# Zero matmuls paced by ScalarE, also into the emptied P.V bank, to a higher count; planned slack behind VectorE, GpSimd and DMA inputs

## Chip, cores, metric

One core of one Trainium2 chip. The metric is device time in microseconds (us) of one execution; lower is better. ACT is ScalarE, DVE VectorE, PE TensorE (PEld its weight loads), POOL GpSimd, SP the engine that issues DMAs.

## The reference, cut

Two identical layers on `x` of 2048 x 512 in bf16, each an attention block with 32 query heads of width 16 and one shared key/value head, followed by a gated MLP with a 2048 x 2048 spatial product.

```python
for layer in range(2):
    x = x + A(layernorm(x))   # q = xn@wq (32 heads), k, v shared; softmax(q k^T / 4) v; @ wo
    x = x + B(layernorm(x))   # z = gelu(xn@w_in); z1, z2 = halves; z1 * (w_sp @ layernorm(z2) + b) @ w_out
```

The softmax needs 2 x 32 x 2048 x 2048 exponentials. That is what ACT does for most of the time.

## The kernel before

The program contains a list scheduler. While it is built it simulates all engines with its own estimates of durations, and emits one fixed order of instructions for each engine, with semaphore waits. At run time an engine that must wait in the middle of its order stops everything behind it.

Scores (QK) are made in "fill" steps of two or three blocks of 128 keys x 512 queries, ACT takes the exponential of two or three blocks at a time from PSUM, and P.V adds them up in one bank, `pvb`. A group is 16 units of four blocks; after it, DVE copies the bank out (`oT`), and only then may the next group write it. Every seventh or eighth block goes to DVE instead of ACT, as a chain of six operations. Projections, MLP and spatial products are side work in two spare banks. Some of it passes through DMA transposes.

Since the attention alone loads PE lightly, the scheduler puts in matmuls of zeros ("zeros" below), so that each window of about 3.4 us has enough columns of work for the clock. These are the parts that matter:

```python
TICK = 3.4133
TICK_COLS = 3060.0
WARM = 800.0
# ... (cut) in the scheduler
    def _arm(self, o):        # when an operation's inputs are all planned
        o.ready = max([d.end if d.eng == "pe" and o.eng == "pe" else d.vis for d in o.deps], default=0.0)
# ... (cut)
    def transpose(self, out, src, deps, sem, pr):
        return self.sc.op("sp", lambda e: e.dma_start_transpose(out, src), 1.2, deps, pr, sem=sem, dma=131072, lat=0.9)
# ... (cut)
class WarmStream:
    def peek(self, f):
        # ... (cut)
        t = sc.below(f, TICK_COLS + WARM)        # first time at which the last window holds fewer columns
        if u >= len(k.units) or k.units[u].first:    # P.V of the next unit would clear the bank
            free = [b for b in sc.banks if not b.busy and not b.closed and b.free_at <= t]
            if not free:
                return None
            self.bank = free[0]
        if not sc.fast(t):
            return (t, -1.0)
        return (t, 0.6)

    def commit(self, t):
        # ... (cut)
        def fn(e):            # adds zero to the P.V bank, or writes zeros to a spare bank
            return e.matmul(k.b32(k.pvb if b is None else b.idx), k.zero[:], k.zero[:, None, :].to_broadcast([P, 4, P]),
                            start=b is not None, stop=b is not None)
        pace = []
        if t > k.sc.free["pe"] + 0.3:
            pace = [d for en in ("act", "dve") for d in k.sc.order[en][-8:] if t - 1.5 < d.vis <= t]
            pace = sorted(pace, key=lambda d: -d.vis)[:1]     # wait for the ACT or DVE operation planned to end last
        o = k.sc.op("pe", fn, 512 / 2400.0, [k.c_zero] + pace + (b.rel if b is not None else []), 9.0, sem="warm")
```

The softmax here doesn't subtract the row's maximum and nothing guards it: scores larger than these inputs give would overflow.

## Time and profile before

| | before |
|---|---|
| timed runs known at the prediction | 1846.22 us median of 3 (1843.32 to 1848.53) |
| the profiled execution, not among them | 1860.4 us, span of the core 1858.4 |
| granted clock in the profiled execution | 0.983 |
| zeros / blocks on DVE | 786 / 514 |

The page of before: busy time of each engine, two of its rows of 40 slices (tenths), the chain that ended last by engine, and two groups. A group's line gives its operation and shapes, then busy us, mean ns of one, and the idle time of its engine just before it.

```profile
span 1858.4 us, 30069 instructions
PE 1599.4 (86%) x11874; PEld 473.0 (25%) x11874; DVE 1700.6 (92%) x2912; ACT 1746.0 (94%) x1570; POOL 52.4 (3%) x90
...
ACT  8999999999999999999569999999999999999983
PEclk9899999999999999998999999999999999999999
...
ACT 39%; DVE 21%; PE 20%; issue 17%; DMA 1%; POOL 1%; ACTq 0%; SPq 0%; POOLq 0%
...
L1374 ACT ACTIVATE Pa<-ps_all 128x1536 bf16<-128x1536 f32 (+1 forms) x1433 | 1631.8, 1372 | 32.6 <-PE ps_all L1694 30.8
...
L1676 PE MATMUL ps_all<-zero 128*128 128x512 bf16 x786 | 257.8, 399 | 34.9 <-DVE mv L1032 7.2
```

ACT is the limit: it is busy 94% of the time, and where its exponentials (L1374) wait, it is for QK (PE, L1694): 30.8 us in all. The rest of its idle time lies at the start, around the middle and at the end.

The windows of before over some of the eleven stretches at half clock. The columns are the stretch, its length, then busy us of PE, PEld, DVE, ACT and POOL with counts, the clock, DMA share and GB/s; the sum is over all eleven.

```profile
core 0: us, PE busy (x) PEld busy (x) DVE busy (x) ACT busy (x) POOL busy (x), PEclk, DMA share, GB/s
...
448.51:455.33 6.82, 6.69 (x27) 1.26 (x28) 3.17 (x6) 3.89 (x3) 1.87 (x2) 0.50 0.00 0
...
1161.89:1165.31 3.42, 3.42 (x17) 0.57 (x16) 2.25 (x4) 1.23 (x2) 0.00 (x0) 0.50 0.39 78
...
sum 64.86, PE 62.84 PEld 11.76 DVE 38.54 ACT 47.14 POOL 4.00; mean PE 5.71 PEld 1.07 DVE 3.50 ACT 4.29 POOL 0.36
```

At half clock PE is full and ACT is not: 47 of 65 us. That each stretch is one, two or three times 3.41 us agrees with the Trainium skill, "TensorE: Matmul & The Clock Gate", Part 1, which gives a free-running window of 3413 ns that decides the clock.

One of these stretches, in the timelines of before's SP queue, PE and ACT from 443 to 456 us (start, length, engine, line, operation; in brackets the idle time before it and what ended it):

```profile
444.53 3.35 SPq L547 DMA_TRANSPOSE xnTB<-xn  x2
...
446.58 0.61 PE L1450 MATMUL ps_all<-Pa,V 128*32 128x512 bf16 x8
448.64 0.93 PE L939 MATMUL ps_all<-w_in_r,xnTB 128*128 128x448 bf16 x2 [1.45 <-DMA xnTB<-xn]
449.50 0.61 PE L1694 MATMUL ps_all<-qs,kT 32*128 32x512 bf16 x3
...
450.16 2.52 ACT L1374 ACTIVATE Pa<-ps_all 128x1536 bf16<-128x1536 f32 x2 [1.70 <-PE ps_all L1694]
453.92 2.54 ACT L1374 ACTIVATE Pa<-ps_all 128x1536 bf16<-128x1536 f32 x2 [1.24 <-PE ps_all L1694]
```

PE reaches a side matmul (L939) whose input comes from a DMA transpose, waits for it, and QK (L1694) stands behind. By then the clock has halved, and ACT waits twice, 1.70 and 1.24 us.

### The profile page before, as it was taken

Reading aid. Unit: us, or ns where it says so; the run is one execution under the profiler, and the core shown is the slowest. Engines: PE = TensorE matmul, PEld = TensorE weight load, DVE = VectorE, ACT = ScalarE, POOL = GpSimd, SP = SyncE. Lnnn points to the kernel's source line nnn. Section 1 sums busy time; section 2 is a strip of 40 time slices with the busy share of each in tenths; the row PEclk is TensorE's granted clock in tenths of the full one; section 3 lists DMA queues with packets and bytes.
Section 4 is the critical chain, followed back from the end, with each engine's and each line's share of the span. In section 5 each row is a group of like instructions: output and inputs, shape, how many; then the busy total and the mean of one; then the engine's idle time right before and its main releaser. Section 6 shows DMA issues by size and latency. Waiting matters only on the chain.

```text
span 1858.4 us, 30069 instructions
## 1 busy us (share of the span) xinstructions
PE 1599.4 (86%) x11874; PEld 473.0 (25%) x11874; DVE 1700.6 (92%) x2912; ACT 1746.0 (94%) x1570; POOL 52.4 (3%) x90
## 2 busy tenths in 40 slices
PE   8878788778899999998887787987887899899998
PEld 3221222122222222222431211221122222222324
DVE  8999999999988999985869999999999998998868
ACT  8999999999999999999569999999999999999983
POOL 2000000000000000000010000000000000000000
PEclk9899999999999999998999999999999999999999
DMA  9700010001000021101120000100010000112013
GB/s 271 200 1 1 9 38 1 1 1 23 17 24 24 24 46 44 47 35 55 48 51 1 1 1 5 42 1 1 1 21 15 29 24 26 44 43 72 10 55 110
DMA packets 122963, 68.02 MB, mean 37 GB/s; under 512 B 76996, under 2 KB 119240, under 8 KB 122824
## 3 DMA queue, kind: packets, MB, share of 16 engines
q1 hardware_dynamic: 121240, 65.95, 13.2%
q8 instruction: 94, 1.54, 0.3%
q14 instruction: 45, 0.37, 0.1%
q10 hardware_dynamic: 1584, 0.16, 0.1%
HBM read 30.97 MB, written 17.83 MB: 26 GB/s over the span
## 4 chain that ended last, share of the span: by engine, by line
ACT 39%; DVE 21%; PE 20%; issue 17%; DMA 1%; POOL 1%; ACTq 0%; SPq 0%; POOLq 0%
ACT Pa L1374 38%; PE ps_all L1694 5%; PE ps_all L1116 5%; DVE E L1558 3%; PE ps_all L1450 3%; DVE Pd L1589 3%; DVE E L1587 2%; DVE E L1583 2%; DVE E L1585 1%; PE ps_all L1676 1%; PE ps_all L1208 1%; DVE st L634 1%; PE ps_all L939 1%; DVE gp L1129 1%; DVE st L1030 1%
## 5 line engine op out<-in xcount | busy, mean ns | idle before, releaser
L1374 ACT ACTIVATE Pa<-ps_all 128x1536 bf16<-128x1536 f32 (+1 forms) x1433 | 1631.8, 1372 | 32.6 <-PE ps_all L1694 30.8
L1694 PE MATMUL ps_all<-qs,kT 32*128 32x512 bf16 x4096 | 567.9, 389 | 186.9 <-ACT Pa L1374 173.2
L1558 DVE TENSOR_SCALAR E<-ps_all 128x512 f32<-128x512 f32 x514 | 351.1, 685 | 32.3 <-PE ps_all L1694 28.9
L1694 PEld LDWEIGHTS ps_all<-qs,kT 32*128 32x128 bf16 x4096 | 139.0, 91 | 751.7 <-ACT Pa L1374 691.2
L1450 PE MATMUL ps_all<-Pa,V 128*32 128x512 bf16 x3582 | 326.3, 391 | 0.0
L1589 DVE SCALAR_TENSOR_TENSOR Pd<-E 128x1024 uint16<-128x1024 f32 x259 | 313.5, 1211 | 4.2
L1676 PE MATMUL ps_all<-zero 128*128 128x512 bf16 x786 | 257.8, 399 | 34.9 <-DVE mv L1032 7.2
L1116 PE MATMUL ps_all<-wsT,z2n 128*128 128x512 bf16 x714 | 200.3, 383 | 1.5 <-DVE E L1558 0.5
L1450 PE MATMUL ps_all<-Pd,V 128*32 128x512 bf16 x514 | 182.4, 391 | 0.0
L1585 DVE TENSOR_TENSOR E<-E 128x1024 f16<-128x1024 f16 x259 | 176.6, 682 | 4.7
L1587 DVE TENSOR_TENSOR E<-E 128x1024 f16<-128x1024 f16 x259 | 176.6, 682 | 4.2
L1583 DVE TENSOR_SCALAR E<-E 128x1024 f16<-128x1024 uint16 x259 | 176.6, 682 | 1.6
L1586 DVE TENSOR_SCALAR E<-E 128x1024 f16<-128x1024 f16 x259 | 107.8, 416 | 2.3
L1676 PEld LDWEIGHTS ps_all<-zero 128*128 128x128 bf16 x786 | 59.8, 98 | 171.4 <-issue 83.5
L1129 DVE TENSOR_TENSOR gp<-ps_all,gp 128x512 f16<-128x512 f32 x112 | 75.8, 686 | 28.4 <-PE ps_all L1116 28.3
L1450 PEld LDWEIGHTS ps_all<-Pa,V 128*32 128x32 bf16 x3582 | 64.4, 94 | 121.9 <-issue 118.1
L1116 PEld LDWEIGHTS ps_all<-wsT,z2n 128*128 128x128 bf16 x714 | 54.1, 97 | 95.6 <-issue 55.1
L796 PE MATMUL ps_all<-xnTA,wq_pad 128*128 128x512 bf16 (+2 forms) x384 | 72.5, 315 | 0.9 <-DVE z1s L986 0.3
L939 PE MATMUL ps_all<-w_in_r,xnTB 128*128 128x448 bf16 x256 | 63.2, 359 | 3.7 <-DMA xnTB<-xn 2.8
L975 PE MATMUL ps_all<-xnTB,w_in_r 128*128 128x512 bf16 (+2 forms) x336 | 62.8, 310 | 1.9 <-DVE gp L986 1.0
L1208 PE MATMUL ps_all<-E 128*128 128x512 bf16 x224 | 53.9, 380 | 3.6 <-ACT E L1187 2.8
L1187 ACT ACTIVATE E<-ps_all 128x512 f16<-128x512 f32 (+1 forms) x49 | 23.7, 555 | 28.6 <-PE ps_all L1175 28.6
(89 smaller groups left out, 996.0 us busy)
## 6 DMA issues: line engine op xcount, KB each, us to landing
wsT_scratch<-gp SPq DMA_DIRECT2D x16, 512.0 KB, 3.6
wsT<-wsT_scratch SPq DMA_DIRECT2D x8, 1024.0 KB, 5.4
z1s<-z_scratch SPq DMA_DIRECT2D x16, 448.0 KB, 3.8
wsT<-wsT_scratch SPq DMA_DIRECT2D x8, 512.0 KB, 3.5
z_scratch<-z1s SPq DMA_DIRECT2D x4, 896.0 KB, 5.2
X<-in_A_x_dram SPq DMA_DIRECT2D x8, 256.0 KB, 5.9
out_dram<-X SPq DMA_DIRECT2D x16, 128.0 KB, 2.0
w_in_r<-in_B_w_in_dram SPq DMA_DIRECT2D x1, 1792.0 KB, 10.3
```

The source lines that it names most:

```text
L1116: ins = e.matmul(self.b32(b), self.z2n[:, s, f * 128:(f + 1) * 128], w_[:, s - s0, :] if s - s0 < na or not spare else wsp[:, s - s0 - na, :],
L1129: return e.tensor_tensor(dst, self.b32(b), dst, ALU.add)
L1374: return e.activation(k.Pa[:, base:base + n, :], k.b32(b0, n).rearrange("p (k q) -> p k q", k=n), ACTF.Exp, scale=SCALE)
L1450: ins = e.matmul(k.b32(k.pvb)[32 * j:32 * j + 32, :], k.V[:, u.kt, 32 * j:32 * j + 32], b.slot, tile_position=(0, 32 * j), start=u.first, ...
L1558: c = k.sc.op("dve", lambda e: e.tensor_scalar(k.ey[:, s, 512 * i:512 * (i + 1)], k.b32(j.bank.idx)[:, 0:512], E_LOG2, E_BIAS, op0=ALU.mul ...
L1583: o2 = sc.op("dve", lambda e: e.tensor_scalar(x, lo, E_X * 2.0 ** -16, E_X * E_A, op0=ALU.mult, op1=ALU.add), d_sb(n, 0.521e-3), self.ops ...
L1585: o3 = sc.op("dve", lambda e: e.tensor_tensor(w, x, x, ALU.mult), d_sb(n, 0.521e-3), [o2, self.wfree], pr)
L1586: o4 = sc.op("dve", lambda e: e.tensor_scalar(w, w, E_C, None, op0=ALU.add), d_sb(n, 0.26e-3), [o3], pr)
L1587: o5 = sc.op("dve", lambda e: e.tensor_tensor(w, w, x, ALU.mult), d_sb(n, 0.521e-3), [o4], pr)
L1589: o7 = sc.op("dve", lambda e: e.scalar_tensor_tensor(po.bitcast(U16), y, E_D, w, op0=ALU.add, op1=ALU.add), d_sb(n, 1.042e-3), [o5] + self ...
L1676: return e.matmul(k.b32(k.pvb if b is None else b.idx), k.zero[:], k.zero[:, None, :].to_broadcast([P, 4, P]), start=b is not None, stop=b ...
L1694: return e.matmul(self.b32(bank), self.kT[32 * j:32 * j + 32, kt * 128:(kt + 1) * 128], self.qs[32 * j:32 * j + 32, g.q.slot, :], tile_pos ...
```

## The change

Its intent: keep the clock up with more zeros, also at the edges of a group, where no bank was free for them; let zeros follow ACT, the limiting engine, and not a late DVE; and plan 0.3 us of slack between a DVE, GpSimd or DMA operation and a side matmul that needs it, so that PE seldom stops in its order. Cut to its core:

```diff
+        sl = SLACK if o.eng == "pe" and o.prio >= 0.9 else 0.0
-        o.ready = max([d.end if d.eng == "pe" and o.eng == "pe" else d.vis for d in o.deps], default=0.0)
+        o.ready = max([... else d.vis + (sl if d.eng in ("dve", "pool", "sp") else 0.0) for d in o.deps], default=0.0)
...
+SLACK = 0.3
+AHEAD = 1200.0
-WARM = 800.0
+WARM = 1200.0
...
-        ... dma_start_transpose(out, src), 1.2, deps, pr, sem=sem, dma=131072, lat=0.9)
+        ... dma_start_transpose(out, src), 1.2, deps, pr, sem=sem, dma=131072, lat=1.4)
...   (GpSimd pow: planned 0.3 + 0.17 n becomes 0.38 + 0.17 n, and 0.3 + 0.23 n in the MLP's layernorm)
-        t = sc.below(f, TICK_COLS + WARM)
+        near = u < len(k.units) and (k.units[u].first or k.units[u].last)
+        t = sc.below(f, TICK_COLS + WARM + (AHEAD if near else 0.0))
...
-            if not free:
-                return None
-            self.bank = free[0]
+            if free:
+                self.bank = free[0]
+            else:
+                ev = k.pv_s.evac
+                if ev is None or ev.start is None or ...:
+                    return None
+                t = max(t, ev.vis)
+                self.bank = k.pv_bank
+                self.bank.rel = [ev]
...
-            pace = [d for en in ("act", "dve") for d in k.sc.order[en][-8:] if t - 1.5 < d.vis <= t]
+            pace = [d for d in k.sc.order["act"][-8:] if t - 1.5 < d.vis <= t] or \
+                [d for d in k.sc.order["dve"][-8:] if t - 1.5 < d.vis <= t]
```

All edits but the pacing also change what the scheduler plans, so the order of the whole program is rebuilt.

More of the change, by code (lines that the diff above doesn't have):

```diff
@@ L157, in _arm @@
     def _arm(self, o):
-        o.ready = max([d.end if d.eng == "pe" and o.eng == "pe" else d.vis for d in o.deps], default=0.0)
+        sl = SLACK if o.eng == "pe" and o.prio >= 0.9 else 0.0
+        o.ready = max([d.end if d.eng == "pe" and o.eng == "pe" else d.vis + (sl if d.eng in ("dve", "pool", "sp") else 0.0) for d in o.deps], default=0.0)
         self.ready[o.eng].append(o)
@@ L511, in __init__ @@
         self.pv_evac = None
+        self.pv_bank = Bank(self.pvb)
         self.load(A_x, A_wq, A_wk, A_wv, A_wo, B_b_sp)
@@ L546, in transpose @@
     def transpose(self, out, src, deps, sem, pr):
-        return self.sc.op("sp", lambda e: e.dma_start_transpose(out, src), 1.2, deps, pr, sem=sem, dma=131072, lat=0.9)
+        return self.sc.op("sp", lambda e: e.dma_start_transpose(out, src), 1.2, deps, pr, sem=sem, dma=131072, lat=1.4)
     def dma(self, fn, deps, sem, nbytes, prio=5.0, eng="sp", issue=0.5):
@@ L641, in ln @@
                                                     self.mhalf[:, 0:1].to_broadcast([P, n]), ALU.pow),
-                  0.3 + 0.17 * n, [a, self.c_mh], pr)
+                  0.38 + 0.17 * n, [a, self.c_mh], pr)
         xo = []
@@ L1037, in mixer_chunk @@
                                                     self.mhalf[:, 0:1].to_broadcast([P, nt]), ALU.pow),
-                  0.3 + 0.17 * nt, [a], pr)
+                  0.3 + 0.23 * nt, [a], pr)
         for t in T:
@@ L1660, in peek @@
         f = max(f, k.c_zero.vis)
-        t = sc.below(f, TICK_COLS + WARM)
+        near = u < len(k.units) and (k.units[u].first or k.units[u].last)
+        t = sc.below(f, TICK_COLS + WARM + (AHEAD if near else 0.0))
         if u >= len(k.units) or k.units[u].first:
             free = [b for b in sc.banks if not b.busy and not b.closed and b.free_at <= t]
-            if not free:
-                return None
-            self.bank = free[0]
+            if free:
+                self.bank = free[0]
+            else:
+                ev = k.pv_s.evac
+                if ev is None or ev.start is None or u >= len(k.units) or k.units[u].grp.layer != k.units[u - 1].grp.layer:
+                    return None
+                t = max(t, ev.vis)
+                self.bank = k.pv_bank
+                self.bank.rel = [ev]
         if not sc.fast(t):
```

## The prediction

> **What bounds the kernel now.** The program plans itself with its own list scheduler; engines run that fixed order. The page gives a span of 1858.4 us, ACT busy 1746.0 (94%), DVE 92%, PE 86%; the chain of waits is 39% ACT exponentials. In undisturbed attention (windows 100-150, 1000-1050, 1200-1250) ACT is busy 50.0 of 50 us: nothing to gain there unless blocks move to DVE. ACT's 112 us of idle time lie, by windows: about 8 at the start, 41 around the layer boundary (850-1000), 36 in the tail after 1800. The latter two are chains of side work that the diff hardly touches. In the list of waits, exponentials wait 30.8 us for the QK matmuls, 52 times: nearly all that the change can win.
>
> **Where those 30.8 us come from.** The granted clock halves eleven times, 65 us in all (mean 0.983). In those stretches ACT idles 17.7 of 65 us; in the 5 us before each, only 0.4 of 55. So PE is too lightly loaded for one activity window (3.41 us, as the Trainium skill, "TensorE: Matmul & The Clock Gate", Part 1, states; the dips last 3.41, 6.83 or 10.24 us, which agrees), the clock halves, the next QK is late. At 151.6, 353 and 448 us the timeline shows no zero matmul for several us: a group's P.V bank waited to be emptied (oT copy on DVE), or PE stood 1.9 us for a DMA transpose. Transposes hold PE also at 233 and 1692 (1.6 us of ACT each).
>
> **What the change does.**
> 1. Zeros to a higher count: +400 columns per window, +1200 more in a group's first and last unit; the emptied bank may be written. Now 786 zeros (about 39 per 50 us in clean attention). +400 columns is 0.8 zeros per window where the limit binds (some 250 windows); +1200 is 2.3 in some 55. I expect 1000 to 1250. One costs about 0.21 us of PE; at 40 of 50 us it has room, and QK keeps priority.
> 2. Pacing by ACT: zeros waited about 90 us for DVE (their line's waits). Those go; little of it reached ACT.
> 3. Planned slack 0.3 us after DVE/GpSimd/DMA, transpose latency +0.5 us, GpSimd pow nearer its measured time (eight columns: 1.96 us measured, planned 1.66, now 2.14): PE stops less on late side inputs. It removes perhaps 3-5 us of ACT idle, and costs perhaps 1-3 us in tail and boundary.
>
> **Sum.** Half-clock time 65 to about 25 us, worth 10-12 us of ACT; late side inputs 3-5; minus 1-3 for slack and zeros in the way. Total about 14 us, under 1%. A 2% gain needs 37 us, more than all those waits together. Further, the plan is rebuilt: the number of DVE blocks (514 now, each worth about 0.43 us of ACT) and the side work's order can shift the time by several us either way.
>
> Predicted 1831 us, 80% range 1816 to 1846. Faster by over 2%: 0.07; within 2%: 0.91; slower: 0.02.
>
> **What would show each step.** Zeros 1000-1250. Mean clock at or above 0.992, at most five dips, none at group boundaries in mid-attention; those left sit at the start (56 us), the gelus and the boundary. Exponentials wait 12-18 us for QK instead of 30.8. Zeros' waits on DVE nearly vanish, on ACT grow. ACT still fully busy in undisturbed attention. DVE blocks 500-528. Tail and boundary idle within 3 us of now.
>
> **What would make it wrong.** Dips that remain because PE starves on a side wait with the zeros behind it in order; zeros delaying QK in its narrow window (many small ACT waits in clean stretches); slack that lets the bank-starved side work slip and lengthens boundary and tail; DVE blocks shifting by over 20.

## The result

| | before | after |
|---|---|---|
| timed, first job | 1845.78 us median of 4 (1843.32 to 1848.53) | 1841.25 us median of 4 (1838.96 to 1843.61) |
| ratio, first job | | 0.9975 (95%: 0.9952 to 0.9998) |
| profiled execution | 1860.4 us, clock 0.983 | 1843.53 us, clock 0.996 |
| half-clock stretches in it | 11, 64.9 us | 4, 13.7 us |
| exponentials wait for QK in it | 30.8 us | 13.5 us |
| zeros / blocks on DVE | 786 / 514 | 1119 / 512 |

Ratios here are the mean time of one kernel's fast runs over that of the other's of the same rounds, so they are not quite the ratio of the medians quoted. The two profiled executions differ by 16.9 us; the medians of the timed ones by 4.5.

The same lines of the page of after:

```profile
span 1841.7 us, 30729 instructions
PE 1634.4 (89%) x12125; PEld 502.7 (27%) x12207; DVE 1698.4 (92%) x2902; ACT 1740.2 (94%) x1564; POOL 51.1 (3%) x90
...
ACT  7999999999999999998569999999999999999983
PEclk9999999999999999999999999999999999999999
...
ACT 44%; PE 24%; issue 19%; DVE 12%; DMA 0%; POOL 0%; ACTq 0%; POOLq 0%; DVEq 0%
...
L1378 ACT ACTIVATE Pa<-ps_all 128x1536 bf16<-128x1536 f32 (+1 forms) x1434 | 1629.7, 1382 | 15.6 <-PE ps_all L1706 13.5
...
L1687 PE MATMUL ps_all<-zero 128*128 128x512 bf16 x1119 | 338.3, 388 | 13.6 <-DVE mv L1036 3.7
```

The exponentials' busy time is unchanged, 1629.7 against 1631.8 us, and their wait for QK fell by 17.3 us. That the span fell by nearly as much, 16.7, is chance: ACT's idle time as a whole (span minus busy) fell by only 10.9 us, from 112.4 to 101.5, and its busy time by 5.8. Other waits of ACT grew: by its list of waits those of the `xnTA` copies from 3.9 to 9.5 us and those of the `kT` copies from 9.1 to 14.5. The windows of after over its four half-clock stretches:

```profile
core 0: us, PE busy (x) PEld busy (x) DVE busy (x) ACT busy (x) POOL busy (x), PEclk, DMA share, GB/s
920.56:923.97 3.41, 3.41 (x20) 1.33 (x20) 3.05 (x10) 1.45 (x1) 0.00 (x0) 0.50 0.00 0
934.21:937.63 3.42, 3.20 (x10) 1.34 (x10) 3.25 (x10) 1.74 (x2) 0.00 (x0) 0.50 0.19 38
1162.91:1166.32 3.41, 3.33 (x14) 1.04 (x15) 2.80 (x5) 1.54 (x2) 0.17 (x1) 0.50 0.00 0
1425.73:1429.14 3.41, 3.41 (x17) 0.68 (x13) 1.81 (x3) 2.59 (x4) 2.46 (x1) 0.50 0.55 183
sum 13.65, PE 13.35 PEld 4.39 DVE 10.91 ACT 7.32 POOL 2.62; mean PE 3.34 PEld 1.10 DVE 2.73 ACT 1.83 POOL 0.66
```

Two lie at the layer boundary (no exponential runs from 865 to 903 us), one in a stretch of gelus (1426); one, at 1163, is in the middle of attention. And the place that answers to 444 us of before, in the timeline of after, all engines from 444 to 450 us:

```profile
444.09 2.50 SPq L551 DMA_TRANSPOSE xnTB<-xn  x2
...
445.88 0.61 PE L1687 MATMUL ps_all<-zero 128*128 128x512 bf16 x2
446.41 0.39 PE L1706 MATMUL ps_all<-qs,kT 32*128 32x512 bf16 x4
446.78 0.39 PE L1687 MATMUL ps_all<-zero 128*128 128x512 bf16 x1
...
449.84 0.36 PE L943 MATMUL ps_all<-w_in_r,xnTB 128*128 128x448 bf16 x1
```

The matmul that needs the transpose (L943) now stands 5.75 us behind its issue, QK and zeros fill the gap, and nothing waits for the transpose.

So the profiles show what the change was meant to do. Open was why the timed runs showed only a third of it.

### The profile page after: what moved, and what is told of

It is laid out like the page before. It is cut to its first block, busy times and chain, and to the rows that moved or that the text cites. A ratio compares the mean times of both kernels' runs of the same rounds, so it can differ in the third digit from the quotient of the medians.

```text
span 1841.7 us, 30729 instructions
## 1 busy us (share of the span) xinstructions
PE 1634.4 (89%) x12125; PEld 502.7 (27%) x12207; DVE 1698.4 (92%) x2902; ACT 1740.2 (94%) x1564; POOL 51.1 (3%) x90
## 4 chain that ended last, share of the span: by engine, by line
ACT 44%; PE 24%; issue 19%; DVE 12%; DMA 0%; POOL 0%; ACTq 0%; POOLq 0%; DVEq 0%
ACT Pa L1378 43%; PE ps_all L1706 6%; PE ps_all L1120 6%; PE ps_all L1454 4%; PE ps_all L1212 2%; PE ps_all L1687 2%; DVE E L1562 2%; DVE st L638 1%; DVE Pd L1593 1%; PE ps_all L943 1%; DVE E L1587 1%; DVE E L1589 1%; DVE E L1591 1%; DVE X L1217 1%; PE ps_all L1117 1%
## 5 line engine op out<-in xcount | busy, mean ns | idle before, releaser
L1378 ACT ACTIVATE Pa<-ps_all 128x1536 bf16<-128x1536 f32 (+1 forms) x1434 | 1629.7, 1382 | 15.6 <-PE ps_all L1706 13.5
L1706 PE MATMUL ps_all<-qs,kT 32*128 32x512 bf16 x4096 | 562.2, 385 | 164.3 <-ACT Pa L1378 148.0
L1687 PE MATMUL ps_all<-zero 128*128 128x512 bf16 x1119 | 338.3, 388 | 13.6 <-DVE mv L1036 3.7
L1120 PE MATMUL ps_all<-wsT,z2n 128*128 128x512 bf16 x655 | 183.7, 382 | 5.8 <-issue 3.5
L1687 PEld LDWEIGHTS ps_all<-zero 128*128 128x128 bf16 x1119 | 85.1, 98 | 183.4 <-issue 118.1
L943 PE MATMUL ps_all<-w_in_r,xnTB 128*128 128x448 bf16 x256 | 64.7, 359 | 0.3 <-DVE E L1562 0.2
L642 POOL TENSOR_SCALAR ve<-mv 128x2 f32<-128x2 f32 (+1 forms) x28 | 10.3, 366 | 1388.2 <-DVE mv L640 1388.0
```

The costliest lines, as they stand in the source:

```text
L1120: ins = e.matmul(self.b32(b), self.z2n[:, s, f * 128:(f + 1) * 128], w_[:, s - s0, :] if s - s0 < na or not spare else wsp[:, s - s0 - na, :],
L1378: return e.activation(k.Pa[:, base:base + n, :], k.b32(b0, n).rearrange("p (k q) -> p k q", k=n), ACTF.Exp, scale=SCALE)
L1706: return e.matmul(self.b32(bank), self.kT[32 * j:32 * j + 32, kt * 128:(kt + 1) * 128], self.qs[32 * j:32 * j + 32, g.q.slot, :], tile_pos ...
```

## The experiments

"Run" below means at least five rounds beside the kernel before on the same chip, and one profile. "Late" is a DMA transpose of activations (there are 68) that landed more than 2.8 us after its issue; punctual ones take 2.4 to 2.5 us.

| label | what | median us | before beside it | ratio (95%) | mean clock of its runs |
|---|---|---|---|---|---|
| before_again | before, unchanged | 1848.75 | 1848.45 | 1.0000 (0.9980 to 1.0020) | 0.991 |
| pace | pacing alone | 1842.82 | 1848.45 | 0.9973 (0.9954 to 0.9992) | 0.993 |
| zeros | all edits of zeros | 1842.12 | 1848.45 | 0.9966 (0.9950 to 0.9981) | 0.997 |
| side | slack and estimates | 1852.70 | 1848.45 | 1.0018 (1.0001 to 1.0034) | 0.989 |
| nop43 | before, in effect | 1851.44 | 1852.82 | 0.9997 (0.9982 to 1.0013) | 0.987 |
| nop86 | before, in effect | 1848.94 | 1852.82 | 0.9986 (0.9969 to 1.0004) | 0.990 |
| nopace | zeros not paced | 1848.13 | 1852.82 | 0.9977 (0.9962 to 0.9992) | 0.986 |
| zeros_oldpace | zeros, old pacing | 1843.83 | 1852.82 | 0.9948 (0.9935 to 0.9962) | 0.998 |
| wait43 | before + 43 empty waits | 1847.00 | 1851.97 | 0.9971 (0.9950 to 0.9991) | 0.992 |
| wait88 | before + 88 empty waits | 1844.28 | 1851.97 | 0.9960 (0.9940 to 0.9980) | 0.991 |
| zwarm | limit 1200, bank, pacing | 1839.05 | 1851.97 | 0.9932 (0.9911 to 0.9953) | 0.996 |
| after_again | after, unchanged | 1841.58 | 1851.97 | 0.9943 (0.9921 to 0.9964) | 0.997 |
| after_w41 | after + 41 empty waits | 1842.52 | 1851.87 | 0.9951 (0.9935 to 0.9968) | 0.996 |
| after_w83 | after + 83 empty waits | 1841.92 | 1851.87 | 0.9951 (0.9935 to 0.9966) | 0.997 |
| zwarm_w41 | zwarm + 41 empty waits | 1838.84 | 1851.87 | 0.9934 (0.9916 to 0.9951) | 0.997 |
| zwarm_w82 | zwarm + 82 empty waits | 1838.75 | 1851.87 | 0.9938 (0.9919 to 0.9958) | 0.995 |
| after_fewer | after with 792 zeros | 1864.41 | 1848.49 | 1.0087 (1.0062 to 1.0113) | 0.964 |
| pvpace | bank and pacing, limit 800 | 1834.25 | 1848.49 | 0.9921 (0.9902 to 0.9941) | 0.995 |

Lines with the same figure for before were run in one job on one chip. All kernels gave correct results.

### Was the first profile typical? (before_again)

No edit.

> The kernel before, unchanged, profiled once more. Theory A (the first profile of before caught an unusually disturbed execution: it took 1860.4 us where the timed ones took 1843 to 1849, so only part of its 30.8 us of exponential waits is there to win in a normal run): this profile shows a span near 1844, a mean clock of 0.988 or more, and exponentials that wait 12 to 22 us for QK. Rival B (those 30 us are in every run, and the change wins them but gives back some 10 us in the layer boundary, the tail or by a worse order): span 1855 or more, clock 0.983, waits 28 to 33 us. Ratio to before 0.999 to 1.001 either way.

The profile again fell on a slow execution (1852.8 us; the six ran from 1844.11 to 1853.33), neither as good as theory A said nor as bad as rival B: clock 0.987, ten stretches of 47.8 us at half clock, and

```profile
ACT Pa L1374 <- PE ps_all L1694: 24.4, 45, 2.2
```

(the list of waits: us in total, times, longest). So executions of before differ widely, and the first profile was at the bad end. (Two later profiles of what turned out to be the same program, nop43 and nop86, have 61.4 and 23.9 us at half clock.) The five jobs timed before 55 times (11 in each): 1850.8 us on average, from 1846.0 to 1858.7, clock from 0.983 to 0.994. The first profile took longer than all of these, and its clock, 0.983, is as low as the lowest of them. Time and clock go together: correlation -0.91, and a least-squares line falls by 10.2 us for 0.01 of clock. 0.01 of mean clock is 37 us at half clock (0.02 x 1850), so one us at half clock goes with 0.28 us of time.

What makes equal executions differ can be seen from the run of pacing below, which has the same order of instructions. At about 350 us PE does the same work in both kernels, to within 0.13 us, up to the moment when in one of them the clock halves. The timelines of PE, before_again first, then pace:

```profile
347.65 0.40 PE L1694 MATMUL ps_all<-qs,kT 32*128 32x512 bf16 x4 [0.95 <-ACT Pa L1374]
348.56 0.39 PE L1694 MATMUL ps_all<-qs,kT 32*128 32x512 bf16 x2 [0.52 <-ACT Pa L1374]
348.88 1.04 PE L1450 MATMUL ps_all<-Pa,V 128*32 128x512 bf16 x7
...
349.86 1.03 PE L1676 MATMUL ps_all<-zero 128*128 128x512 bf16 x2
```

```profile
347.77 0.40 PE L1695 MATMUL ps_all<-qs,kT 32*128 32x512 bf16 x4 [0.95 <-ACT Pa L1374]
348.69 0.39 PE L1695 MATMUL ps_all<-qs,kT 32*128 32x512 bf16 x2 [0.52 <-ACT Pa L1374]
349.00 0.61 PE L1450 MATMUL ps_all<-Pa,V 128*32 128x512 bf16 x7
...
349.55 0.61 PE L1676 MATMUL ps_all<-zero 128*128 128x512 bf16 x2
```

Seven P.V matmuls take 1.04 us in one and 0.61 in the other. The load before is equal; what differs is the place of the windows over it. In each profile the stretches at half clock begin on one grid of 3.41 us, and the grid's offset changes from execution to execution. On that grid, PE is busy 1.95 us in the window before the halving of before_again (345.46 to 348.88), and 2.34 us in pace's window there (344.87 to 348.28), which kept the clock. In the other profiles of the same program the figure is 1.94 (before) and 1.95 (nop43), which halved, and 2.18 (nop86), which did not. It is no sharp limit: over the 20 profiles, from 60 to 1780 us, 79 of the 158 full-clock windows with under 2.0 us of busy PE were followed by a halving, and 9 of the 9473 with 2.3 us or more.

### Parts of the change (pace, zeros, side)

`pace` is only the last hunk of the diff. It leaves the plan, and so every engine's order, as it was. `zeros` has all hunks of the zeros; `side` has the slack, the transpose's latency and the pow estimates.

> Before, with only the pacing of zero matmuls changed to ScalarE first. The order of all instructions stays that of before; only the semaphores that zeros wait for change. Theory A: pacing hardly matters, ratio 0.998 to 1.001, clock as before, the zeros' waits on DVE fall from about 90 to under 40 us. Rival C (waits of the zeros on a late VectorE were what starved PE and let the clock fall): clock 0.994 or more, ratio 0.995 to 0.997.

> Before with all edits to the zero matmuls (limit 1200, 1200 more at group edges, emptied bank, pacing) and no slack, transpose or pow estimate. Theory A: about 1100 zeros, clock 0.995 or more, at most 4 dips, exponentials wait 8 to 16 us for QK; time 1837 to 1844, ratio 0.995 to 0.999: all of the gain. Rival D (the planned slack brings the gain, since PE stalled in order on side inputs): ratio 0.999 to 1.002.

> Before with only the planned slack of 0.3 us, the transpose latency and the pow estimates; zeros as before. Theory A: no gain; clock 0.983 to 0.992 as before; the later side products lengthen the plan, ratio 1.000 to 1.008. Rival D (slack brings the gain): ratio 0.995 to 0.998 and PE's waits for DMA transposes gone.

Pacing alone won 5.9 us (means 1843.8 and 1849.7), more than theory A allowed, at a clock that was little better (0.993 against 0.990, about 2.5 us by the line above). All zero edits together won 7.2 us (1842.6), and did raise the clock. Slack and estimates alone cost 2.5 us (1852.2): rival D fell. They did what they were meant to do, since PE's waits for the transposes of attention and MLP came down to 1.3 us (in before_again 8.5 us on weight loads alone, by the list of waits of PEld). It gained nothing: the rebuilt plan is no better and the clock was not helped. Much of the cost stands at the start: in all six profiles with this hunk (side, and the five of after's order) the first exponential starts at 16.4 us or later, in the 14 others at 14.4; in side PE waits there 1.56 us for `xn` from DVE. The transposes that were late changed too (19 of them), so 2.5 us is not the price of slack alone.

Pacing had passed its test, but for which reason? Since before_again and pace have the same order, each exponential can be set against its twin. They run in step to about 0.01 us, and differ by jumps. The largest jumps in favour of pace lie at 446 to 450 us (3.5 us) and at 1157 us (2.2 us). At both, PE in before_again waited for a late transpose, and in pace the same transpose came in time: issued at the same moment of the plan, 4.31 and 4.00 us to landing in one, 2.42 each in the other. No wait of a zero was involved.

The late transposes had something in common. The trace holds TensorE's instruction fetches: 94 packets of 16,384 bytes on queue q8. (In before 11,874 loads, as many matmuls and 480 waits make 258 instructions for each.) In the first six profiles, most late transposes had met a fetch (by the rule given below 68 of 85 late ones and 22 of 323 punctual ones; the first text of the next section counts with a wider window). Pacing adds 105 separate wait instructions to TensorE's stream, and so moves every later fetch.

### Moving the fetches (nop43, nop86, nopace, zeros_oldpace)

```diff
+                    for _ in range(43 if k == "pe" else 0):    # 86 in the other
+                        e.nop(nofuse=True)
                     for f in prog:
```

`nopace`: `if t > k.sc.free["pe"] + 0.3:` becomes `if False:`. `zeros_oldpace`: `zeros` without the pacing hunk.

> Before, with 43 do-nothing instructions at the head of TensorE's stream; nothing else changes, not even what waits for what. Theory E (the pacing run won because its 105 more wait instructions moved the 8 KB instruction fetches[...], and those fetches delay the DMA transposes that they meet: in six profiles 75 of 85 late transposes met one, and 47 of 323 punctual ones): other transposes are late than the 13th and 41st (late in both profiles of before), and the time moves by 2 to 6 us either way, ratio outside 0.999 to 1.001. Rival C (pacing by ScalarE helps as such): the same transposes late, ratio 0.999 to 1.001.

> The same with 86 do-nothing instructions[...]. Theory E: again another set of late transposes, and a time 2 to 6 us from that of before or of the run with 43. Rival C: ratio 0.999 to 1.001, same set.

> Before, with no pacing of zeros at all: they start as soon as TensorE reaches them. Order of instructions as before, but fewer waits (so the fetches move too). If pacing is what keeps the clock up, zeros bunch ahead and the clock falls: 0.960 to 0.985, more than 12 dips, ratio 1.002 to 1.010. If pacing waits only cost PE time: clock as before, ratio 0.996 to 0.999. If only the fetches matter (theory E): clock 0.985 to 0.994, ratio 0.996 to 1.004.

> All edits of the zero matmuls except pacing by ScalarE (zeros paced by ScalarE or VectorE as before); no slack or estimates. About 1100 zeros in the order of the run with all edits of the zeros. If the higher count carries the gain: clock 0.995 or more, ratio 0.995 to 0.998. If pacing by ScalarE carries it: clock 0.990 or less, ratio 0.998 to 1.001.

The 8 KB in these texts is my misreading, put right in the next section. The first two failed as experiments: the do-nothing instructions were dropped at the build (TensorE still had 12356 in the trace, and the fetches stayed where they were). They count as two more runs of before, and show what such a run can do by chance: -0.1 and -2.1 us. Without any pacing the kernel was 4 us faster than before although its clock was lower. That fits two of the three forecasts, that pacing costs PE time and that the fetches matter; the comparison in the next section decides for the fetches. Its stream has 106 more separate waits than before, nearly as many as pace has, and the same transposes were late as in pace, but for a few (24, 25 and 29 in pace alone, 31 and 44 here alone). So it is hardly whom a zero waits for that made pace faster. And with the old pacing the zero edits won 9.1 us (1843.1 against 1852.2): pacing by ACT adds nothing that can be seen to a higher count.

### The fetches again, with real instructions (wait43, wait88)

```diff
+        if o.eng == "pe" and okey == "warm" and o.start > 60.0 and extra[0] > 0:
+            more = [(sems[e_].h, 1) for e_ in ("pool", "act", "dve")]      # passed long ago
...
+            for (h_, v_) in more:
+                e.wait_ge(h_, v_)
```

> The do-nothing instructions of the two earlier runs turned out to be dropped at the build (TensorE's instruction count stayed 12356), so theory E was not tested. This is before with 43 more real instructions on TensorE: waits for long-passed semaphore values, ahead of zeros after 60 us. Nothing else changes. Theory E (the place of the 8 KB instruction fetches decides which DMA transposes are late): counted from 0, the late transposes 2, 3, 12, 18, 19, 40, 54 and 65 of before become punctual, and others, among 4, 7, 27, 28, 29, 67, become late (worked out from the fetch times in the trace, moved by 43/128 of a period); the time moves by 2 to 6 us either way. Rival F (the late ones are tied to the work around them, and DVE waits of the zeros make them late): the same transposes late as in before, ratio 0.999 to 1.001.

> The same with 88 more waits. Theory E: late ones among 10, 22, 23, 48, 49, 53, and 12, 18, 19, 40, 54, 65 punctual. Since then none that holds TensorE in the middle of attention may be left, I expect ratio 0.995 to 0.999. Rival F: the same late ones as in before, ratio 0.999 to 1.001.

Waits that wait for nothing made the kernel 5.1 and 7.1 us faster (means 1846.3 and 1844.3 against 1851.4). Rival F fell, and theory E holds in its main point: in both runs transposes 2, 3, 12, 18, 19, 40, 41, 54 and 55 became punctual (65, forecast too, stayed late). Which ones would become late I had wrong in both runs (none of the six places forecast for each became late), because I took a fetch for 8 KB and 128 instructions. It is 16 KB; the trace counts a load and its matmul once among TensorE's records, so 128 records are 256 instructions (255 to 258 for each fetch in the 20 profiles). With a period of 256, 43 waits should hit 0, 1, 5, 16, 17, 21, 30, 34, 35, 45, 57, 58, 61, 64; late were 0, 1, 5, 16, 17, 20, 21, 24, 25, 30, 31, 56, 57, 60, 65. That is 8 of the 14, and it was worked out after the run.

Could the added waits have helped in another way, say by delaying zeros? Before_again, pace, nopace, wait43 and wait88 run the same exponentials in the same order, so each can be set against its twin. From 440 to 453 us all four others gain 4.0 us on before_again, and from 1150 to 1159 us 2.4 us; in all four the transposes of these places (12 and 40) landed after 2.40 to 2.43 us. In before, nop43 and nop86, the program of before_again itself, they took 3.89 us or more, and the gains are 0.1, 1.4 and 2.7 us, and -0.1, 1.5 and 1.3: there the same transposes were late, and what differs is, as far as seen, the clock. So these gains stand where a transpose became punctual.

The place at 1150 us, in the timelines of all engines, before_again and then wait88:

```profile
1150.32 6.04 SPq L547 DMA_TRANSPOSE onT<-on  x4
...
1152.78 0.61 PE L1676 MATMUL ps_all<-zero 128*128 128x512 bf16 x2
...
1154.75 1.49 PE L907 MATMUL ps_all<-wo_r,onT 128*128 128x512 bf16 x3 [1.36 <-DMA onT<-on]
...
1156.17 1.03 PE L1694 MATMUL ps_all<-qs,kT 32*128 32x512 bf16 x5
...
1156.82 1.45 ACT L1374 ACTIVATE Pa<-ps_all 128x1536 bf16<-128x1536 f32 x1 [2.15 <-PE ps_all L1694]
```

```profile
1146.42 5.12 SPq L556 DMA_TRANSPOSE onT<-on  x4
...
1148.89 0.60 PE L1685 MATMUL ps_all<-zero 128*128 128x512 bf16 x2
...
1149.55 0.81 PE L916 MATMUL ps_all<-wo_r,onT 128*128 128x512 bf16 x3
1150.29 0.93 PE L1703 MATMUL ps_all<-qs,kT 32*128 32x512 bf16 x5
```

The order is the same. In before_again the fetch began at 1151.5 us, 1.2 us after the first transpose; the transpose landed after 4.00 us, PE stood 1.36 us, the clock halved, and ACT waited 2.15 us. In wait88 the fetch had begun at 1140.6 us, 5.8 us ahead of the transpose, which took 2.40 us; ACT waited for nothing.

Over the 20 profiles, with one rule for all (a fetch that begins between 0.3 us before and 2.3 us after the issue): of 204 transposes that met a 16 KB fetch 181 were late; of 94 that met only one of 8 KB (queue q14) 33; of 1062 that met none 40.

### Does the change depend on that place? (zwarm, after_again, after_w41, after_w83, zwarm_w41, zwarm_w82)

`zwarm` is before with `WARM = 1200.0`, the hunk of the emptied bank and that of pacing, without `AHEAD`, slack and estimates. The others add empty waits as above.

> Before with the limit at 1200, the emptied bank and pacing by ScalarE, but without the further 1200 columns at group edges and without slack and estimates. About 970 zeros. If the raised limit does the work: clock 0.994 or more, and a time as with all edits of the zeros or better by up to 4 us, 1836 to 1843, ratio 0.992 to 0.997. If the group edges are what loses the clock: 0.990 to 0.993 and ratio 0.997 to 0.999.

> The changed kernel, unaltered, beside the others on one chip. Theory A: clock 0.995 to 0.998, ratio 0.994 to 0.998, equal within 2 us to the run with all edits of the zeros (0.9966 on its chip), that is, slack and estimates bring nothing. Rival D (slack brings part): better than the zeros alone by 3 us or more, ratio under 0.995.

> The changed kernel with 41 more passed waits on TensorE[...], as in the runs with 43 and 88 that made before 5 and 7 us faster. Theory G (before lost 5 to 7 us to an unlucky place of the fetches, and the changed kernel, with slack behind the transposes and more zeros, no longer depends on it): within 2 us of the changed kernel, 1839 to 1844, ratio to before 0.993 to 0.996, clock 0.995 or more. Rival H (the changed kernel was merely lucky in its place too): 1844 or more, ratio 0.997 or more.

> The same with 83 more waits[...]. Theory G: again 1839 to 1844 and within 2 us of the run with 41. Rival H: the two differ by 4 us or more.

> The best version so far (limit 1200, emptied bank, pacing; no slack, no further columns at group edges) with 41 more waits. If slack is what makes a kernel independent of the fetches: this one moves by 3 us or more from 1839. If the higher zero count does it alone (a late transpose then costs only its own wait, not two windows at half clock): 1837 to 1842, ratio 0.992 to 0.996, clock 0.994 or more.

> The same with 82 more waits. Count alone: 1837 to 1842, within 3 us of the one with 41. Slack needed: 1842 or more in at least one of the two.

On this chip the change is worth 10.2 us (1841.2 against 1851.4), ratio 0.9943, twice what the first job showed. The ratio met rival D's test (under 0.995), the time theory A's: it is within 2 us of zeros (1842.6, on the same chip), and before was 1.7 us slower in this job. Since zeros_oldpace reached 0.9948 without slack, and slack alone lost time, rival D is not supported. With the fetches moved it keeps its time, 1842.0 and 1842.0; so does zwarm, 1839.1, then 1838.9 and 1839.6. Before, moved in the same way, went over 7 us. (With 256 instructions to a fetch, 41 and 83 waits are about a sixth and a third of its distance; other places were not tried.) Theory G's times hold, and rival H fell. But slack, which theory G named, is not what makes the kernel independent: zwarm has none, in zwarm_w41 17 transposes were late (15 in before_again), and its time stayed. Late transposes cost little here, where the clock stays up:

```profile
PEld ps_all L917 <- DMA onT<-on: 2.2, 3, 1.2
...
ACT Pa L1384 <- PE ps_all L1711: 12.6, 35, 1.6
```

(the list of waits of zwarm_w41: PE's weight loads still wait 2.2 us for these and 6.0 us for all transposes, where before_again had 9.3; ACT waits 12.6 us for QK, where before_again had 24.4.) zwarm was 2.1 us better than the change beside it, and 2.3 and 3.2 with like numbers of waits in the next job; so the group-edge columns, slack and estimates together seem to cost about that (each pair's intervals overlap). The first exponential, 2.0 us later with slack and estimates, is a cost of that size.

### Count or order? (after_fewer, pvpace)

`after_fewer` keeps after's order and waits, and emits three of every ten zeros after 20 us as a bare semaphore step. `pvpace` is before with the emptied bank and the pacing alone, 770 zeros.

> The changed kernel with its order, slack and waits kept, but three of every ten zeros after 20 us replaced by their bare semaphore step: 792 zeros are left of 1119, about as many as before. If the higher count is what keeps the clock up: clock 0.986 to 0.993, six dips or more, time 1844 to 1850, ratio 0.996 to 0.999. If slack and the new order carry the gain: 1839 to 1843, ratio 0.993 to 0.995, though the clock falls.

> Before with the emptied bank and pacing by ScalarE only; limit 800 as before, about 770 zeros. If the count is what matters: clock 0.988 to 0.994, time 1841 to 1847, and slower than the version with limit 1200 (1839) by 2 us or more. If the emptied bank or the order built with it is the gain: 1836 to 1840 and clock 0.995 or more.

With its order and slack but 792 zeros, the changed kernel is 16.3 us slower than before (1865.6 against 1849.3), further than I expected: 28 stretches at half clock, in attention above all. Late transposes are not the reason: it had 8, the profile of after 12. Two lines of its page:

```profile
PEclk9998998989999999999999989999998999998999
...
L1379 ACT ACTIVATE Pa<-ps_all 128x1536 bf16<-128x1536 f32 (+1 forms) x1434 | 1634.1, 1335 | 34.6 <-PE ps_all L1711 32.4
```

So in this order it is the zeros that keep the clock. The run overstates the price of a lower count, since I took zeros from places where the plan had counted on them; before has 786, placed for that count.

pvpace refuted the other half of my expectation. With the count of before it was the fastest kernel of all, 1835.4 us on average, 13.9 under before. The line fitted to before gives 1844.8 us at its clock of 0.995, so by this estimate (0.995 is just outside the fitted range) some 9 us of this are not clock. Its page shows where the clock and the waits stand:

```profile
PEclk9999999999999999999999999999999999999999
...
L1375 ACT ACTIVATE Pa<-ps_all 128x1536 bf16<-128x1536 f32 (+1 forms) x1434 | 1628.0, 1397 | 15.0 <-PE ps_all L1702 13.8
```

The emptied bank rebuilds the plan, and with it moves the fetches; which of the two gives the 9 us is not shown. Moving the fetches alone can do about half: wait88, in before's order, lies 5 us below the same line (1844.3 us at 0.9905). And pvpace's profile has 9 late transposes, that of before_again 15. ACT's idle time was 94.8 us in it and 95.5 in wait88's. Whether pvpace keeps its time when the fetches move was not tried, and its lead on zwarm (0.9921 against 0.9932 to 0.9938, on different chips, intervals overlapping) is not shown. Both beat before and after.

## Why the prediction was right or wrong

Predicted 1831 us, from 1846: 15 us less, of which the sum gives 14. Measured in the first job: 1841.25, 4.5 us less. The time is inside the range; the gain was forecast three times too large. Its repetition beside 11 runs of before gave 10.2 us. So part of the miss is the sample of before, and the first job's interval (0.9952 to 0.9998) and the second's (0.9921 to 0.9964) overlap.

- **"Half-clock time 65 to about 25 us, worth 10-12 us of ACT": this is the term that was mis-sized.** The rate was right (0.28 us of time for each us at half clock, here fitted over 55 runs; 0.25 to 0.3 in the prediction). The 65 us were not. They come from one execution of 1860.4 us, longer than any of the 55 and with a clock as low as the lowest, while I subtracted from timed runs around 1846. By the fitted line (an estimate) a run of 1845.8 us has a clock of 0.994, which is 22 us at half clock. The profile of after has 13.7. The difference of 8 us is worth 2.3 us, not 10 to 12. For the average of 55 runs (0.989, 40 us at half clock) it is 26 us or 7.3.
- **"Exponentials wait 30.8 us ... nearly all that the change can win"** has the same fault; before_again had 24.4. It has another: between the two profiles that wait fell by 17.3 us, as forecast, but ACT's idle time by only 10.9, since other waits of ACT grew. The contradiction was in front of me: the profiled execution was 14 us slower than the median I used.
- **Planned slack, "It removes perhaps 3-5 us of ACT idle, and costs perhaps 1-3 us in tail and boundary": wrong in sign.** With the estimates it cost 2.5 us alone (1.0018, 1.0001 to 1.0034), though it did remove PE's waits on transposes. And the cost stands elsewhere: at the start, where the first exponential slid by 2.0 us.
- **"Pacing by ACT ... little of it reached ACT": right in its mechanism, with a surprise.** Pacing alone was worth 5.9 us, but so were 43 and 88 empty waits (5.1 and 7.1); what pacing changed was the place of the instruction fetches. I knew nothing of that cause of lateness when I named "late side inputs". It also came out that zeros still wait for DVE: in after their largest waits on it (9.3 and 8.4 us) are in side work; "nearly vanish" was too much.
- **Right:** 1000 to 1250 zeros (1119); clock at or above 0.992 (0.996) and at most five dips (4), in the places named but for one, 1163 us, where PE stood for a DVE copy (`qs`); waits for QK 12 to 18 us (13.5); ACT fully busy in undisturbed attention (50.00 of 50 us from 100 to 150); DVE blocks 500 to 528 (512); boundary and tail within 3 us (the longest break between exponentials 37.4 against 39.7, the tail 55.1 against 54.3).
- **"The plan is rebuilt ... can shift the time by several us either way"**: agrees with pvpace, about 9 us beyond its clock, nearly as large as the largest term that I had costed. How much of it is plan and how much the place of the fetches is not shown.

The changed kernel is better mainly because its clock stays up, so that neither an unlucky window nor a late transpose costs several us. In its order the zeros do this, as after_fewer shows; that it needs so many is not shown, since pvpace reached a clock of 0.995 with 770. Before was also unlucky with its fetches: moving them alone won 5 to 7 us, as much as the first measured gain. How the 10.2 us of the repetition divide between clock and fetches is not shown.

## What to carry to other kernels

A profile is one execution: set its time and clock beside those of the timed runs before subtracting anything found in it from their median. When an edit helps that should not matter, add the same number of empty instructions to the old kernel and see whether that helps as much; in a long unrolled program, instruction fetches can delay your DMA transposes. And where a scheduler rebuilds the whole order, an edit's own gain and the luck of the new plan come mixed, so move something harmless and see which part stays. (I did not do that for pvpace, the fastest kernel here.)

## What the Trainium skill lacked or had wrong

- "Runtime: NRT & Kernel Launch", section "Instruction fetch mechanics", says that instructions stream in blocks of 16 KiB (256 instructions) by DMA and that the cost is "mostly hidden". The size agrees (94 packets of 16,384 bytes, 258 instructions each). It lacks that a fetch can delay DMA transposes under way: 181 of 204 that met one landed late (half of them after 3.4 to 4.1 us, where punctual ones took 2.4 to 2.5), against 40 of 1062 that met none, and moving the fetches alone changed this kernel's time by 5 to 7 us.
- "DMA: Bandwidth & Descriptors", section "Rules for kernel authors", says of a transpose next to ordinary DMAs that it "needs nothing". The row is about correct results, and there the runs agree (all were right). It says nothing of time: a transpose that was late with a fetch typically took about 1 to 1.7 us longer, as above.
- "TensorE: Matmul & The Clock Gate", Part 1, calls the place of the free-running window variable from run to run, and says that for modeling the ramp is under 1% of a typical kernel and that one should not fit a count of cold matmuls. It does not say what this does to a long kernel some of whose windows are lightly loaded: equal executions of before ranged from 1846.0 to 1858.7 us, with a correlation of -0.91 between time and mean clock.
- No page says that a do-nothing instruction on TensorE can be dropped at the build: 43 and 86 of them at the head of the stream left the count at 12356 and moved no fetch.
